# Attention backward: dQ in two 256-column matmuls, all of dS turned by the DMA crossbar, dQ half a group later

## The chip, the cores and the metric

The kernel runs on one core of a Trainium2 chip. The metric is the time of one execution on the device in microseconds (us), forward and backward in one launch; the median of repeated runs is compared. A profiled execution gives a trace of every instruction of the core's engines: TensorE (PE; its weight loads are PEld), VectorE (DVE), ScalarE (ACT), GpSimd (POOL) and SyncE (SP, which only issues DMAs here).

## What is computed

The function is one transformer block with adaptive layer norm (S = 2048 tokens, D = 512, 32 heads of 16) and its whole gradient. The outputs are the block's output and the gradients of the input, the weights and the conditioning vector. Cut to what matters here, the attention is

```python
scores = jnp.einsum('bhqd,bhkd->bhqk', q, k) * scale
p = _softmax(scores, axis=-1)
o = jnp.einsum('bhqk,bhkd->bhqd', p, v)
```

and its gradient is taken by `jax.vjp`. With dP the product of dO and V, the backward forms dS = p * (dP - rowsum), then dK = dS^T Q, dV = p^T dO and dQ = dS K. The change concerns dQ and the turning of dS that it needs.

## The kernel before

The program has three stretches: the forward with the backward of the MLP (0 to 1170 us), the attention backward (`attn_bwd`, L1429, 1170 to 2401 us) and the closing weight gradients and input gradient (`phase6`, to 2522 us). Only the second and the start of the third are touched.

**Loops.** `attn_bwd` walks over 8 quads of heads (g), 2 pairs of heads in each (jp), 4 chunks c of 512 keys and 16 blocks ib of 128 queries. Four query blocks make a group (G = 4), so a pair has 16 groups and the whole has 256. One step is one query block for the two heads a = 0, 1 of a pair. Queries are on the partitions, the 512 keys along the free dimension.

**One step** issues, for each head: the scores (L1584) into a PSUM tile `st` (three buffers); dP of the step before (`dP`, L1509) into a PSUM tile `dp` (three buffers); ScalarE's exponential of `st` into `pu` (L1587); and VectorE's product of `dp` and `pu` into the dS tile (L1513). The scores and dP use different halves of TensorE's rows. The dS tile `dsg` holds a group: 128 x (4 steps, 2 heads, 512 keys), from a pool of three buffers (L1354).

**The hand-over.** In every second group (`off`, L1515: the odd ones) the tile of step 1, head 1 isn't multiplied by VectorE: ScalarE copies `dp` to SBUF (L1521) and GpSimd multiplies (L1522). So VectorE has 7 products in an odd group and 8 in an even one.

**Batches.** After the two st and dP pairs of a step TensorE does a batch of older work: after odd steps dK and dV of two steps (`kv`, L1455: 8 matmuls of 512 columns on four column tiles), after even steps dQ of four units (`dq`, L1478). A unit of dQ is one 128-key block of one head of one group. For it, K's 32 columns (two heads' place, one of them zero) are the weights and the turned dS is the moving operand:

```python
for i in range(G):
    nc.tensor.matmul(accq[32 * i:32 * i + 32, ib0 // G, :], lhsT=T["K"][:, 4 * c + sub, col:col + 32],
                     rhs=dsT[:, (i * 2 + a) * 4 + sub, :],
```

So the four query blocks of a group lie on four strips of 32 PSUM partitions, and the group's number along the free dimension. All chunks accumulate in one PSUM tile `accq`.

**Turning dS.** `dsT` holds the group's 32 blocks of 128 x 128 with keys on the partitions (four buffers, L1355). In an odd group the DMA crossbar turns all 32 (`dma_start_transpose` on SyncE's queue, L1530, issued when the group's last product is issued). In an even group `turn_ds` (L1535) has TensorE transpose the first four blocks into an `st` buffer (L1543) and ScalarE copy them out (L1544), and the crossbar turns the other 28.

**When dQ runs.** `dS` appends 8 units to `pendq` when a group is complete. After an even step, four units are popped if more than 16 wait (eight if more than 24, L1595). In steady state 24 wait at a group's first step, so a batch reads a dsT whose turning was issued two groups before.

**The end of a pair.** With the pair's last unit, `dq` has VectorE scale `accq` into `dqT` (L1483) and appends a turn to `turnq`. A turn is popped at step 1 of a group (L1578), one in each: first two for dK and dV (`turn`, L1468 and L1472), then the one for dQ (`turn_q`, L1491: four transposes; L1492: one ScalarE copy). The last pair's rest is done after the loops (L1601 to L1629), among the first matmuls of the weight gradients.

The order on TensorE, SyncE and GpSimd in this stretch is the order of the code; nothing reorders it. GpSimd's queue also issues the loads of the next pair's operands (L1573), each behind a small copy (L1572) that paces it. `keep` (L1366) is a buffer of 128 x 8192: its first 2048 columns hold K of the even quads, and in the last pair all of it is filled with the normalised input for the weight gradients.

Of the kernel before, what the change touches and what calls it, by code (L numbers as in the profile page):

```python
# [9 lines left out]
BF16 = mybir.dt.bfloat16  # L10
F32 = mybir.dt.float32
ACT = mybir.ActivationFunctionType
ALU = mybir.AluOpType
# [6 lines left out]
P = 128  # L20
DH = 16
# [84 lines left out]
class K:  # L106
# [1230 lines left out]
    def phase5(self):  # L1337
        S, D, NQ, ST, DT = self.S, self.D, self.NQ, self.ST, self.DT
        nc, io = self.nc, self.io
        opa = self.open_pool("p56a", bufs=1)  # L1340
        self.pup = self.open_pool("p5pu", bufs=6)
        self.dq_t = opa.tile([P, ST, D], BF16, name="dq_t")
        self.dk_t = opa.tile([P, ST, D], BF16, name="dk_t")
        self.dv_t = opa.tile([P, ST, D], BF16, name="dv_t")
        self.opa = opa
        self.junk6 = opa.tile([P, D], F32, name="junk6")
        nc.gpsimd.memset(self.dsa_part[:], 0.0)
        assert ST * self.H == D
        self.cs = [self.csq[:], self.rl[:].rearrange("p s h -> p (s h)"), self.mod_25[:, 1, :]]
        self.parts = [self.dq_t, self.dk_t, self.dv_t]  # L1350
        self.stp = self.open_pool("p5st", bufs=3, space=PSUM)
        self.dpp = self.open_pool("p5dp", bufs=3, space=PSUM)
        self.kvp = self.open_pool("p5kv", bufs=1)
        self.dsp = self.open_pool("p5ds", bufs=3)  # L1354
        self.dtp = self.open_pool("p5dt", bufs=4)  # L1355
        self.accp = self.open_pool("p5acc", bufs=1, space=PSUM)
        self.attn_bwd()
# [71 lines left out]
    def attn_bwd(self):  # L1429
# [12 lines left out]
        accp = self.accp  # L1442
        acckv = accp.tile([P, 512], F32, name="acckv")
        nc.vector.memset(acckv[:], 0.0)
        accq = accp.tile([P, ST // G, P], F32, name="accq")
        masked, kvs = self.masked, self.kvs
        pend, pendq, turnq = [], [], []

# [25 lines left out]
        def dq(u):  # L1474
            (T, g, jp, c, ib0, a, sub, dsT) = u
            col = 32 * (2 * jp + a) - DH * a
            for i in range(G):
                nc.tensor.matmul(accq[32 * i:32 * i + 32, ib0 // G, :], lhsT=T["K"][:, 4 * c + sub, col:col + 32],  # L1478
                                 rhs=dsT[:, (i * 2 + a) * 4 + sub, :],
                                 start=(c == 0 and ib0 == 0 and a == 0 and sub == 0), stop=False,  # L1480
                                 skip_group_check=True)
            if (c, ib0, a, sub) == (SC - 1, ST - G, 1, 3):
                nc.vector.tensor_scalar(self.dqT[:], accq[:].rearrange("p b q -> p (b q)"), self.scale, None, ALU.mult)  # L1483
                turnq.append((g, jp, None, 0))

        def turn_q(g, jp):

            h0 = 4 * g + 2 * jp
            tp = stp.tile([P, ST // G, P], BF16, name="st")
            for b in range(ST // G):  # L1490
                nc.tensor.transpose(tp[:, b, :], self.dqT[:, b * P:(b + 1) * P], self.ident[:])  # L1491
            nc.scalar.copy(self.dq_t[:, :, h0 * DH:(h0 + 2) * DH], tp[:].rearrange("p b (i e) -> p (b i) e", i=G))  # L1492

        def kv_two(n=2):
            for u in pend[2 - n:2]:
# [19 lines left out]
        def off(c, ib):  # L1515
            return (c * SC + ib // G) % 2 == 1
# [7 lines left out]
        def dS(u):  # L1524

            (T, g, jp, c, ib, kvT, pu, dsg, i, grp) = u
            pend.append((T, g, jp, c, ib, kvT, pu, dsg[:, i]))
            if i == G - 1:
                dsT, n = grp
                nc.sync.dma_start_transpose(dsT[:, n:, :], dsg[:].rearrange("p i a k -> p (i a k)")[:, n * P:])  # L1530
# [17 lines left out]
        last = None  # L1548
        for g in range(NQ):
            for jp in range(2):  # L1550
                if jp == 0:
# [14 lines left out]
                for c in range(SC):  # L1566
                    c0 = 512 * c
                    for ib0 in range(0, ST, G):
                        m = c * (ST // G) + ib0 // G
                        while pieces and (total - len(pieces)) * SC * ST <= m * G * total:  # L1570
                            if last:
                                nc.gpsimd.tensor_copy(tick[:], last[7][0:1, 0, 0, 0:1])  # L1572
                            nc.gpsimd.dma_start(*pieces.pop(0))  # L1573
                        dsg, grp = self.dsp.tile([P, G, 2, 512], BF16, name="ds"), []
                        for i in range(G):
                            ib = ib0 + i
                            q = slice(ib * P, (ib + 1) * P)
                            if turnq and i == 1:  # L1578
                                turn(*turnq.pop(0))
                            pu = self.pup.tile([P, 2, 512], BF16, name="pu")  # L1580
                            for a in range(2):
                                stt = stp.tile([P, 512], F32, name="st")
                                rs = slice(64 * jp, 64 * jp + 64)
                                nc.tensor.matmul(stt[:], lhsT=T["QT"][rs, q], rhs=masked["KT"][a][rs, c0:c0 + 512],  # L1584
                                                 start=True, stop=True)
                                held = dP(last, a) if last else None
                                nc.scalar.activation(pu[:, a, :], stt[:], ACT.Exp, scale=self.scale)  # L1587
                                if held is not None:
                                    dP_pool(last, held)
                            if last:  # L1590
                                dS(last)
                            last = (T, g, jp, c, ib, kvT, pu, dsg, i, grp)
                            if i % 2 == 1 and len(pend) >= 4:
                                kv_two()
                            elif i % 2 == 0 and len(pendq) > 4 * G:  # L1595
                                for _ in range(8 if len(pendq) > 6 * G else 4):
                                    dq(pendq.pop(0))
                            if i == 2:
                                turn_ds(dsg, grp, off(c, ib))
            T = Tn  # L1600
        with tc.manual_schedule(engines=ALL):  # L1601
            for t in (2, 0):
# [339 lines left out]
```

## Time and profile before

| what | value |
|---|---|
| median of three runs | 2524.97 us (2520.79 to 2530.05) |
| the profiled execution, its span | 2524.31 us, 2522.4 us |
| mean granted TensorE clock | 0.998 |
| stretch 1170 to 2401 us: PE, DVE, ACT, POOL busy | 1192.3, 1186.4, 1207.2, 317.1 us of 1231 |
| GB/s of the DMAs in that stretch | 222 |
| crossbar issues (L1530), landing after min / median / max | 256; 5.3 / 7.1 / 10.2 us |
| ScalarE copies of turned blocks (L1544) | 128, 605 ns each |

In lines of groups the first number after the bar is the busy time in us, the second the mean length of one in ns; then comes the idle time of the engine just before them and what ended most of it. Lengths of neighbouring instructions overlap, since an engine starts one before the last has fully ended: the distance from start to start is the cost, not the length. For the same reason matmul busy time says little about how full TensorE is. Lines of the timeline give start, length from the first start to the last end, engine, code line, operation, operands and how many were merged. Everything that the prediction costs is in the stretch from 1170 to 2401 us and in the first 15 us behind it.

### The profile page before, as it was taken

The numbers are of one execution on the slowest core, as the hardware profiler recorded it, in microseconds if no ns is written. First come the engines' busy times: TensorE is split into PE (matmuls) and PEld (weight loads), VectorE is DVE, ScalarE is ACT, GpSimd is POOL, SyncE is SP. The second block draws the span as 40 slices with busy tenths as digits, with TensorE's granted clock in tenths as the row PEclk, the third lists the DMA queues.
The fourth block names the chain that finished last, engine by engine and source line by source line (L and its number), as shares of the span: only waits on it lengthen the run. The fifth ranks groups of instructions, "written<-read, shape, count | busy, mean of one in ns | idle before, by whom it ended". The sixth has DMA issues, their size and how long they took to land.

```text
span 2522.4 us, 76903 instructions
## 1 busy us (share of the span) xinstructions
PE 2433.1 (96%) x30791; PEld 1107.9 (44%) x30791; DVE 1705.4 (68%) x3519; ACT 2296.2 (91%) x3773; POOL 713.9 (28%) x1289
## 2 busy tenths in 40 slices
PE   8999999999999999989999999999999999999998
PEld 4555555555555554673333333333333333333343
DVE  6222223422332343667999999999999999999957
ACT  7999999999999997535999999999999999999945
POOL 2344531321131022255222222222222222222223
PEclk9999999999999999999999999999999999999999
DMA  4589761441343044699999999999999999999997
GB/s 167 134 178 202 179 114 64 116 99 44 103 118 74 24 137 129 139 191 214 234 221 218 218 226 220 223 227 218 219 218 223 225 221 221 222 228 226 237 211 198
DMA packets 1260558, 446.30 MB, mean 177 GB/s; under 512 B 1204052, under 2 KB 1228246, under 8 KB 1260198
## 3 DMA queue, kind: packets, MB, share of 16 engines
q1 hardware_dynamic: 1219654, 336.29, 70.7%
q0 software_dynamic: 38464, 104.04, 13.9%
q8 instruction: 241, 3.95, 0.7%
q10 hardware_dynamic: 2080, 1.05, 0.1%
q14 instruction: 119, 0.97, 0.1%
HBM read 75.83 MB, written 64.49 MB: 56 GB/s over the span
## 4 chain that ended last, share of the span: by engine, by line
PE 59%; ACT 22%; DMA 11%; issue 4%; DVE 3%; SPq 1%; POOL 0%; DVEq 0%; ACTq 0%; POOLq 0%
ACT pu L391 18%; PE st L1584 17%; DMA dsT<-ds 8%; PE acckv L1455 8%; PE st L388 8%; PE accq L1478 5%; PE accbank L322 3%; PE dp L1509 3%; ACT pu L1587 2%; PE dps L1050 2%; PE pps L1237 2%; PE dps L995 1%; DVE ds L1513 1%; PE st L1543 1%; PE pps L631 1%
## 5 line engine op out<-in xcount | busy, mean ns | idle before, releaser
L1513 DVE TENSOR_TENSOR ds<-dp,pu 128x512 bf16<-128x512 f32 x1920 | 1178.3, 681 | 44.5 <-PE dp L1509 26.4
L1587 ACT ACTIVATE pu<-st 128x512 bf16<-128x512 f32 x2048 | 1073.9, 641 | 39.4 <-PE st L1584 21.3
L391 ACT ACTIVATE pu<-st 128x1024 bf16<-128x1024 f32 x992 | 912.2, 1077 | 5.4 <-PE st L388 5.1
L388 PE MATMUL st<-QTm,KTq 128*128 128x512 bf16 x1984 | 588.4, 377 | 19.7 <-ACT pu L391 6.1
L322 PEld LDWEIGHTS <-pu 128*128 128x128 bf16 x8192 | 347.2, 96 | 236.2 <-issue 3.2
L322 PE MATMUL accbank<-Vaug,pu 128*128 128x17 bf16 x8192 | 357.6, 171 | 1.2 <-ACT Vaug L522 0.9
L1509 PE MATMUL dp<-kvm,q 64*128 64x512 bf16 x1024 | 356.4, 382 | 2.2 <-DVE g2w L1056 0.7
L1509 PE MATMUL dp<-kvm,dOTg 64*128 64x512 bf16 x1024 | 356.2, 382 | 0.9
L1584 PE MATMUL st<-kvm,QTg 64*128 64x512 bf16 x1024 | 327.2, 381 | 10.5 <-ACT pu L1587 7.4
L1584 PE MATMUL st<-kvm,q 64*128 64x512 bf16 x1024 | 326.6, 380 | 10.8 <-ACT pu L1587 7.6
L388 PEld LDWEIGHTS <-KTq 128*128 128x128 bf16 x1984 | 188.2, 96 | 177.5 <-issue 125.9
L1522 POOL TENSOR_TENSOR ds<-junk,pu 128x512 bf16<-128x512 f32 x64 | 73.7, 1151 | 378.6 <-DVE ds L1513 336.7
L1522 POOL TENSOR_TENSOR ds<-csq,pu 128x512 bf16<-128x512 f32 x64 | 73.8, 1154 | 356.6 <-ACT csq L1521 356.6
L302 POOL DMA_DIRECT2D QTm<-QTq_d x124 | 63.5, 514 | 342.7 <-PE st L388 321.3
L1455 PE MATMUL acckv<-ds,Qg 128*16 128x512 bf16 x1024 | 154.3, 381 | 0.0
L1455 PE MATMUL acckv<-pu,dOg 128*16 128x512 bf16 x1024 | 154.2, 381 | 0.0
L1455 PE MATMUL acckv<-pu,q 128*16 128x512 bf16 x1024 | 154.0, 381 | 0.0
L1455 PE MATMUL acckv<-ds,q 128*16 128x512 bf16 x1024 | 154.0, 381 | 0.0
L329 DVE RECIPROCAL rl<-accbank 128x4 f32<-128x4 f32 x128 | 22.9, 179 | 159.5 <-PE accbank L322 159.2
L1584 PEld LDWEIGHTS <-q 64*128 64x128 bf16 x1024 | 58.1, 94 | 137.9 <-issue 104.5
L1584 PEld LDWEIGHTS <-QTg 64*128 64x128 bf16 x1024 | 57.7, 94 | 137.7 <-issue 102.7
L1509 PEld LDWEIGHTS <-q 64*128 64x128 bf16 x1024 | 88.4, 93 | 64.2 <-issue 47.4
(387 smaller groups left out, 3138.6 us busy)
## 6 DMA issues: line engine op xcount, KB each, us to landing
KTq<-KTq_d POOLq DMA_DIRECT2D x24, 512.0 KB, 3.8
duT_d<-auT POOLq DMA_DIRECT2D x3, 1792.0 KB, 8.2
aT_d<-rT POOLq DMA_DIRECT2D x3, 1792.0 KB, 11.6
KTq_d<-KTq SPq DMA_DIRECT2D x32, 128.0 KB, 2.0
QTq_d<-ev_fm SPq DMA_DIRECT2D x32, 128.0 KB, 3.4
ktm_d<-ev_tm POOLq DMA_DIRECT2D x32, 128.0 KB, 2.5
VTq_d<-vT POOLq DMA_DIRECT2D x4, 1024.0 KB, 5.8
dsT<-ds SPq DMA_TRANSPOSE x256, 7.1
```

What stands on the lines that cost most here:

```text
L302: nc.gpsimd.dma_start(QTm[j][32 * j:32 * j + 32, :], self.QTq_d[g, 32 * j:32 * j + 32, 512 * qc:512 * (qc + 1)])
L322: nc.tensor.matmul(acc[:, a, sub, :], lhsT=pu[:, a, sub * P:(sub + 1) * P], rhs=Vaug[:, kb, h, :], start=(kb == 0 and a == 0 and sub == 0) ...
L388: nc.tensor.matmul(stt[:, a, :], lhsT=KT[:, kb * P:(kb + 1) * P], rhs=QTm[2 * jp + a][:], start=True, stop=True)
L391: nc.scalar.activation(pu[:], stt[:], ACT.Exp, scale=self.scale)
L1050: nc.tensor.matmul(pt[:], lhsT=a[st], rhs=g_tm[:, st, :], start=(st == 0), stop=(st == ST - 1))
L1455: nc.tensor.matmul(acckv[r:r + DH, :], lhsT=T[n][:, ib, col:col + DH], rhs=src[:, a, :], start=(ib == 0), stop=(ib == ST - 1))
L1478: nc.tensor.matmul(accq[32 * i:32 * i + 32, ib0 // G, :], lhsT=T["K"][:, 4 * c + sub, col:col + 32], rhs=dsT[:, (i * 2 + a) * 4 + sub, :], ...
L1509: nc.tensor.matmul(dp[:], lhsT=T["dOT"][rd, ib * P:(ib + 1) * P], rhs=masked["VT"][a][rd, 512 * c:512 * (c + 1)], start=True, stop=True)
L1513: nc.vector.tensor_tensor(dsg[:, i, a], dp[:], pu[:, a, :], ALU.mult)
L1522: nc.gpsimd.tensor_tensor(dsg[:, i, 1], f[:], pu[:, 1, :], ALU.mult)
L1584: nc.tensor.matmul(stt[:], lhsT=T["QT"][rs, q], rhs=masked["KT"][a][rs, c0:c0 + 512], start=True, stop=True)
L1587: nc.scalar.activation(pu[:, a, :], stt[:], ACT.Exp, scale=self.scale)
```

## The change

dQ's matmuls take 256 columns: two matmuls for each unit, each with two query blocks. Their place in `accq` follows: with b the group's number in the chunk, partitions 32 x (2 x (b mod 2) + h) and columns 256 x (b // 2). `turn_q` copies out in two parts accordingly. The crossbar turns all 32 blocks of every group except in the last pair, where even groups still go by TensorE and ScalarE. The dS tiles become a ring of three tiles and a fourth that lies in `keep`, behind K; in the last pair only the three are used. The bounds for popping dQ units rise from 16 and 24 to 20 and 28.

```diff
-        self.dsp = self.open_pool("p5ds", bufs=3)
+        dsp = self.open_pool("p5ds", bufs=1)
+        self.ds_ring = [dsp.tile([P, 8 * 512], BF16, name=f"ds{k}")[:] for k in range(3)]
+        self.ds_ring.append(self.keep[:, ST * P:ST * P + 8 * 512])
...
-        accq = accp.tile([P, ST // G, P], F32, name="accq")
+        accq = accp.tile([P, 512], F32, name="accq")
...
-            for i in range(G):
-                nc.tensor.matmul(accq[32 * i:32 * i + 32, ib0 // G, :], lhsT=T["K"][:, 4 * c + sub, col:col + 32],
-                                 rhs=dsT[:, (i * 2 + a) * 4 + sub, :],
-                                 start=(c == 0 and ib0 == 0 and a == 0 and sub == 0), stop=False,
+            b = ib0 // G
+            for h in range(2):
+                r, o = 32 * (2 * (b % 2) + h), 256 * (b // 2)
+                nc.tensor.matmul(accq[r:r + 32, o:o + 256], lhsT=T["K"][:, 4 * c + sub, col:col + 32],
+                                 rhs=dsT[:].rearrange("p (i w) k -> p i w k", i=G)[:, 2 * h:2 * h + 2, 4 * a + sub, :],
+                                 start=(c == 0 and b < 2 and a == 0 and sub == 0), stop=False,
...
-            nc.scalar.copy(self.dq_t[:, :, h0 * DH:(h0 + 2) * DH], tp[:].rearrange("p b (i e) -> p (b i) e", i=G))
+            for h in range(2):
+                nc.scalar.copy(self.dq_t[:, 8 * h:8 * h + 8, h0 * DH:(h0 + 2) * DH].rearrange("p (s i) e -> p s i e", i=2),
+                               tp[:, 2 * h:2 * h + 2, :].rearrange("p i (s e) -> p s i e", s=G))
...
-                        dsg, grp = self.dsp.tile([P, G, 2, 512], BF16, name="ds"), []
+                        ring = self.ds_ring[:3] if (g, jp) == (NQ - 1, 1) else self.ds_ring
+                        dsg, grp = ring[n_ds % len(ring)].rearrange("p (i a k) -> p i a k", i=G, a=2), []
+                        n_ds += 1
...
-                            elif i % 2 == 0 and len(pendq) > 4 * G:
-                                for _ in range(8 if len(pendq) > 6 * G else 4):
+                            elif i % 2 == 0 and len(pendq) > 5 * G:
+                                for _ in range(8 if len(pendq) > 7 * G else 4):
                                     dq(pendq.pop(0))
                             if i == 2:
-                                turn_ds(dsg, grp, off(c, ib))
+                                turn_ds(dsg, grp, (g, jp) != (NQ - 1, 1) or off(c, ib))
```

More of the change, by code (lines that the diff above doesn't have):

```diff
@@ L1476, in dq @@
             col = 32 * (2 * jp + a) - DH * a
-            for i in range(G):
-                nc.tensor.matmul(accq[32 * i:32 * i + 32, ib0 // G, :], lhsT=T["K"][:, 4 * c + sub, col:col + 32],
-                                 rhs=dsT[:, (i * 2 + a) * 4 + sub, :],
-                                 start=(c == 0 and ib0 == 0 and a == 0 and sub == 0), stop=False,
+            b = ib0 // G
[4 more added lines that the diff above has]
+                                 start=(c == 0 and b < 2 and a == 0 and sub == 0), stop=False,
                                  skip_group_check=True)
             if (c, ib0, a, sub) == (SC - 1, ST - G, 1, 3):
-                nc.vector.tensor_scalar(self.dqT[:], accq[:].rearrange("p b q -> p (b q)"), self.scale, None, ALU.mult)
+                nc.vector.tensor_scalar(self.dqT[:], accq[:], self.scale, None, ALU.mult)
                 turnq.append((g, jp, None, 0))
@@ L1529, in dS @@
                 dsT, n = grp
-                nc.sync.dma_start_transpose(dsT[:, n:, :], dsg[:].rearrange("p i a k -> p (i a k)")[:, n * P:])
+                nc.sync.dma_start_transpose(dsT[:, n:, :], dsg.rearrange("p i a k -> p (i a k)")[:, n * P:])
                 for a in range(2):
@@ L1547, in attn_bwd @@
         T = self.T0
-        last = None
+        last, n_ds = None, 0
         for g in range(NQ):
```

## The prediction

> **What bounds the kernel now.** I read the page first, for the shares and the groups; then the busy times of the stretch that the diff touches; then the waits of that stretch; then single stretches of the timeline, engine by engine. The profiled execution took 2524.3 us, 2522.4 of it in the span; the median of the three runs is 2525.0, so a sum made on the profile carries over as it is. The backward attention lies between 1170 and 2401 us. The page's groups, with busy time and mean length of one (engine and operation named):
>
> ```profile
> L1513 DVE TENSOR_TENSOR ds<-dp,pu 128x512 bf16<-128x512 f32 x1920 | 1178.3, 681 | 44.5 <-PE dp L1509 26.4
> L1587 ACT ACTIVATE pu<-st 128x512 bf16<-128x512 f32 x2048 | 1073.9, 641 | 39.4 <-PE st L1584 21.3
> ```
>
> VectorE's product is busy for 1178.3 us of these 1231 and idle for 44.5 us in all. The reader should see that nothing that spares ScalarE or TensorE work can bring more than those 44.5 us. The waits between 1176 and 2401 us (waiting line, what ended the wait, total, times, longest):
>
> ```profile
> DVE ds L1513 <- PE dp L1509: 26.4, 62, 2.0
> PE st L1584 <- ACT pu L1587: 14.9, 44, 0.5
> PE accq L1478 <- DMA dsT<-ds: 13.8, 22, 2.1
> DVE ds L1513 <- ACT pu L1587: 3.1, 11, 0.3
> ```
>
> VectorE waits almost only for TensorE's dP, hardly for ScalarE. The timeline of VectorE gives its pace: five products in a stretch with nothing in the way, then five around the tile that ScalarE and GpSimd take over (two answers, start and length first):
>
> ```profile
> 1797.74 3.07 DVE L1513 TENSOR_TENSOR ds<-dp,pu 128x512 bf16<-128x512 f32 x5
> ...
> 1800.73 3.39 DVE L1513 TENSOR_TENSOR ds<-dp,pu 128x512 bf16<-128x512 f32 x5
> ```
>
> One product lasts 0.68, so the first line is (3.07 - 0.68) / 4 = 0.598 us from start to start; the second loses 3.39 - 3.07 = 0.32. Two groups (one with the hand-over, one without) have 15 products: 15 x 0.598 = 8.97, plus 0.31 is 9.28 us. The crossbar's issues on SyncE repeat at just this distance:
>
> ```profile
> 1883.28 4.06 SPq L1530 DMA_TRANSPOSE dsT<-ds  x1
> ...
> 1888.02 3.59 SPq L1530 DMA_TRANSPOSE dsT<-ds  x1
> ...
> 1892.57 4.01 SPq L1530 DMA_TRANSPOSE dsT<-ds  x1
> ```
>
> 1892.57 - 1883.28 = 9.29. So the steady loop is VectorE plus 0.31. Where the 0.31 comes from is in TensorE's timeline:
>
> ```profile
> 1800.87 0.37 PE L1509 MATMUL dp<-kvm,q 64*128 64x512 bf16 x1
> 1801.17 0.41 PE L1478 MATMUL accq<-dsT,keep 128*32 128x128 bf16 x16
> ...
> 1801.51 0.39 PE L1509 MATMUL dp<-kvm,q 64*128 64x512 bf16 x1
> ...
> 1802.06 0.37 PE L1509 MATMUL dp<-kvm,q 64*128 64x512 bf16 x1
> 1802.36 0.39 PE L1455 MATMUL acckv<-ds,q 128*16 128x512 bf16 x2
> ...
> 1802.91 0.39 PE L1509 MATMUL dp<-kvm,q 64*128 64x512 bf16 x1
> ```
>
> A dQ batch (16 matmuls) takes 1801.51 - 1801.17 = 0.34 us of TensorE, a dK/dV batch (8 of 512 columns) 0.54. The dP at 1800.87 is the handed-over tile; the next dP stand behind the dQ batch, behind a dP buffer (1802.06) and behind the dK/dV batch (1802.91), and VectorE starts on each about 0.52 after it (1801.51 to 2.03).
>
> **What the Trainium skill says.** "TensorE: Matmul & The Clock Gate", Part 3 (The mechanism): column tiles of 32 run at once, each with its own weights. The trace agrees: 16 matmuls of 128 columns pass in 0.34 us. The same page, Back-to-back issue gap: N / 2.4 + 2.5 ns, so 56 ns for 128 columns and 109 for 256. The trace: 4 rounds in 0.34, 57 each with 0.11 around them. "DMA: Bandwidth & Descriptors", Latency and other measured facts: 261 GB/s for a DMA transpose; here 32 blocks of 32,768 bytes in 4.06 us are 258. "VectorE: DVE Perf Modes", Why PSUM operands drop a tier: fp32 from PSUM goes at one element a cycle, which fits 0.598 for 512, and no part of the diff changes that.
>
> **The change part by part.**
> *dQ in 256 columns.* Before, the four matmuls of a unit sat on four column tiles; now two matmuls of a unit use two tiles (rows 64 x (b mod 2) onwards), and all units of a batch have the same b. So a batch of 4 units streams 4 x 256 = 1024 columns after each other, as the dK/dV batch does: 0.54 instead of 0.34, +0.20 us in 512 batches, 102 us of TensorE. In the steady loop I put it against the recurrence above. X is the product whose end frees the buffer of the handed-over dP (start 1800.13). The first dP behind the batch would start at X + 1.58 instead of X + 1.38, its product at X + 2.10; but the third product behind it waits for X + 1.20 (the last before the hand-over) + 0.73 (its buffer free) + 0.30 + 0.54 (dK/dV batch) + 0.52 = X + 3.29 today, and by the new path for 2.10 + 2 x 0.598 = X + 3.30. A tie: the loss stays at 0.31. TensorE's sum for two groups is 8 x 0.535 (st and dP) + 4 x 0.54 + 4 x 0.54 = 8.6 of 9.28. Cost 0; if its cover goes, at most the whole 102; if a batch costs 0.02 more, 128 x 0.02 = 3. A gain is excluded, since TensorE only gets more.
> *The crossbar turns all.* 120 groups lose 4 transposes (0.33 of TensorE each) and a ScalarE copy that moves the next exponential by 0.46. ScalarE's sum for two groups falls from 16 x 0.477 + 2 x 0.46 = 8.55 to 8.09, both under 9.28: 0 in the steady loop. Around a pair's end, where the dK/dV copies crowd ScalarE, it may give 0 to 0.8 us; TensorE's longer batches stand in the same place, so I take 0.2 x 15 = -3. SyncE gets 4 blocks more in every second group, 4.06 against 3.59: 0.5 us per two groups, 8.1 of 9.28 where nothing disturbs.
> *Half a group later, fourth buffer.* A batch reads its dsT after 2.5 groups (11.6 us) instead of 2 (9.3); landings take 5.3 to 10.2. The 13.8 us of waits for the crossbar, in about eight spells, each get 2.3 us of credit, but in these spells (issues up to 5.2 us, with loads beside them) 4/60 more is moved, some 200 us x 0.067 = 13 us. Net -1, from -14 to +12. No VectorE wait for a dS buffer is in the trace: 0 for the buffer.
> *A new wait.* Before, the last dQ batch of a pair stood in the third group of the next pair, VectorE's scaling of accq followed in the crowd there, and the four transposes of dqT came three steps later:
>
> ```profile
> 1799.12 0.40 PE L1491 MATMUL st<-ident,dqT 128*128 128x128 bf16 x4
> ...
> 1799.45 0.39 PE L1509 MATMUL dp<-kvm,q 64*128 64x512 bf16 x1
> ```
>
> Now the last batch falls on the first step of the fourth group, and the transposes are popped in the very next step: in the changed program's order on TensorE they stand directly behind the last eight dQ matmuls. TensorE must wait until VectorE, with up to three dP tiles in front, has scaled accq; behind it in TensorE's queue stand the next st and dP, so VectorE runs dry. From the scaling's start: 0.73 until TensorE goes on (as from X to 1800.87), 0.33 for the transposes, 0.52 until the next product: 1.58, of which 0.60 is the scaling itself, done before too. Loss 1.0 us, at 15 ends of pairs: +15. Less is possible if VectorE catches up through the 0.8 above; more if ScalarE runs dry too (1.3).
> *Tail.* 28 units are left instead of 24, at 0.107 instead of 0.057: 3.0 - 1.4 = +1.6, on TensorE, which VectorE's last scaling waits for. dq_t in two copies instead of one: a tenth, 0.
> Sum: 0 - 3 - 1 + 15 + 1.6 = +12.6, 2524.3 + 12.6 = 2537.
>
> **Rivals.**
> A: the credit takes away all waits for the crossbar, 13.8: 2524.3 + 15 - 3 + 1.6 - 13.8 = 2524. For it: the longest wait is 2.1, under 2.3. Against: the spells are fed by more blocks.
> B, the faster side: ScalarE is the bound (91% busy on the page, TensorE waits 44 times for it). Then 120 x 0.46 = 55 go, and 2524.3 - 55 + 16.6 = 2486. It decides if the dP waits of VectorE come from st buffers held by ScalarE; only 14.9 us of TensorE's waits say so, and 8.55 is under 9.28.
> C: the crossbar becomes the bound in a third of the loop (43 double groups): at the disturbed pace of 9.9 us for 60 blocks, 4 more are 0.66: 28 on top of the waits and the tail, less what TensorE's wait gives back: 2524.3 + 28 + 5 = 2557.
> D: the longer batches are not covered: half of 102 shows, 2524.3 + 51 + 13.6 = 2589. Against: 8.6 under 9.28.
>
> **How the numbers follow.** My forecast (2528 to 2547) 0.52, A 0.20, B 0.11, C 0.12, D 0.05. About 0.3%, 7.6 us, is what a measurement can tell from no change. Slower by more: C, D and 0.44 of the forecast, 0.61; within: A but for 0.03, and the rest of the forecast, 0.25; faster: B and 0.03 of A, 0.14. The range leaves out B, D and a little of C and A: 2517 to 2553.
>
> **What would show it.** Right: the crossbar's issues still 9.28 apart for two groups; dQ batches of 0.54; once in each pair VectorE idle for about 1 us ahead of its first product of the fourth group, with TensorE waiting for VectorE at the transposes of dqT; few waits of accq for the crossbar. Wrong: a steady distance of 9.0 (ScalarE had mattered), or over 9.4 (batches or crossbar uncovered); no idle time at the transposes; waits of accq for dsT over 14 us.

## The result, and the profile after

The changed kernel takes 2563.19 us (median of four runs, 2562.92 to 2563.97), the kernel before 2523.49 in the runs beside it. The ratio is 1.0153 with a 95% interval of 1.0136 to 1.0171: slower by 1.5%, some 39 us. The forecast was 2537, +12.6. The direction is right; the size is three times what was forecast, and 2563 lies outside the forecast's range of 2517 to 2553.

The profiled execution has a span of 2561.7 us against 2522.4 before, so it shows the same 39 us, and it shows them in the stretch of the attention backward. An issue is one `dma_start_transpose` on SyncE's queue, and its length is the time that it holds this queue. From one crossbar issue to the issue 16 groups later (one pair of heads) the 15 first pairs take 79.7 us each, 76.9 before; 15 x 2.88 = 43. The last pair, where TensorE still turns a part, takes 72.2 us from its first issue to its last (73.0 before), and the first issue of all comes 3.0 us earlier in this trace: 43.2 - 0.8 - 3.0 is the 39 again.

The page's groups of the changed kernel (busy us, mean ns of one, then idle time before them). VectorE's product now has two rows, since the fourth buffer is called keep:

```profile
L1595 ACT ACTIVATE pu<-st 128x512 bf16<-128x512 f32 x2048 | 1085.7, 612 | 78.9 <-PE dp L1515 23.5
L1519 DVE TENSOR_TENSOR ds<-dp,pu 128x512 bf16<-128x512 f32 x1500 | 913.8, 680 | 44.1 <-PE dp L1515 34.7
...
L1519 DVE TENSOR_TENSOR keep<-dp,pu 128x512 bf16<-128x512 f32 x420 | 262.7, 681 | 49.7 <-PE dp L1515 44.8
```

One product is as long as before (0.68), but VectorE is idle for 44.1 + 49.7 = 93.8 us ahead of them, where it was 44.5. Half of it is ahead of the 420 products into keep, a fifth of all. The waits between 1170 and 2440 us (total, times, longest):

```profile
DVE keep L1519 <- PE dp L1515: 44.8, 59, 2.0
DVE ds L1519 <- PE dp L1515: 34.7, 86, 1.2
PEld L1495 <- DVE dqT L1487: 26.3, 15, 1.8
PE accq L1482 <- DMA dsT<-ds: 25.5, 32, 1.7
...
PE st L1495 <- DVE dqT L1487: 22.1, 15, 1.5
...
PE accq L1482 <- DMA dsT<-keep: 5.8, 11, 1.4
...
PE st L1592 <- ACT pu L1595: 0.7, 3, 0.3
```

Two things are new to TensorE: it waits for the scaling of dqT once in each of 15 pairs, up to 1.8 us, as forecast; and it waits for the crossbar 25.5 + 5.8 = 31.3 us, 13.8 before. The crossbar's own row says why. All issues on SyncE, by source (shortest, median and longest in ns), the kernel before first:

```profile
L1530 SPq DMA_TRANSPOSE dsT<-ds x256: 3419/4113/5953, 1176.1 to 2401.8; - x128
```

```profile
L1536 SPq DMA_TRANSPOSE dsT<-ds x196: 3517/4410/6452, 1173.1 to 2441.2; - x196
L1536 SPq DMA_TRANSPOSE dsT<-keep x60: 4882/5458/6605, 1187.7 to 2363.6; - x60
```

The shortest of the 60 issues that read the fourth buffer, 4.9 us, is longer than the median of the others, 4.4. Over the first 240 groups the mean issue grew from 4.20 to 4.86 us, and the issues fill 97.6% of the time, 87.4% before. In the timeline they stand end to end (start, length):

```profile
1799.42 4.71 SPq L1536 DMA_TRANSPOSE dsT<-ds  x1
...
1804.23 5.30 SPq L1536 DMA_TRANSPOSE dsT<-keep  x1
...
1809.62 14.01 SPq L1536 DMA_TRANSPOSE dsT<-ds  x3
```

1799.42 + 4.71 = 1804.13, and the next one starts 0.1 us later. So by this trace SyncE's queue, that is the crossbar, sets the pace; the experiments test it. The forecast had this as rival C, in a third of the loop; it is nearly the whole.

### The profile page after: what moved, and what is told of

The parts are those of the page before. It is cut to its first block, busy times and chain, and to the rows that moved or that the text cites. A ratio compares the mean times of both kernels' runs of the same rounds, so it can differ in the third digit from the quotient of the medians.

```text
span 2561.7 us, 67535 instructions
## 1 busy us (share of the span) xinstructions
PE 2455.1 (96%) x26215; PEld 1078.3 (42%) x26215; DVE 1705.2 (67%) x3519; ACT 2277.2 (89%) x3669; POOL 715.8 (28%) x1289
## 3 DMA queue, kind: packets, MB, share of 16 engines
q1 hardware_dynamic: 1281094, 352.02, 74.1%
q0 software_dynamic: 38464, 104.04, 13.8%
## 4 chain that ended last, share of the span: by engine, by line
PE 57%; ACT 19%; DMA 17%; DVE 3%; issue 3%; POOL 1%; SPq 0%; DVEq 0%; ACTq 0%; POOLq 0%
ACT pu L391 17%; PE st L1592 15%; DMA dsT<-ds 12%; PE st L388 8%; PE accq L1482 8%; PE acckv L1457 8%; PE accbank L322 3%; PE dp L1515 2%; DMA dsT<-keep 2%; PE dps L1050 2%; PE pps L1237 2%; PE dp L1643 1%; DVE ds L1519 1%; PE pps L631 1%; PE st L1738 1%
## 5 line engine op out<-in xcount | busy, mean ns | idle before, releaser
L1519 DVE TENSOR_TENSOR ds<-dp,pu 128x512 bf16<-128x512 f32 x1500 | 913.8, 680 | 44.1 <-PE dp L1515 34.7
L1592 PE MATMUL st<-kvm,QTg 64*128 64x512 bf16 x1024 | 313.5, 381 | 0.9 <-ACT pu L1595 0.5
L1592 PE MATMUL st<-kvm,q 64*128 64x512 bf16 x1024 | 313.5, 382 | 0.5 <-ACT pu L1595 0.3
L1519 DVE TENSOR_TENSOR keep<-dp,pu 128x512 bf16<-128x512 f32 x420 | 262.7, 681 | 49.7 <-PE dp L1515 44.8
L1482 PE MATMUL accq<-dsT,keep 128*32 128x256 bf16 x2048 | 157.1, 275 | 16.1 <-DMA dsT<-ds 12.4
L1482 PE MATMUL accq<-dsT,Kg 128*32 128x256 bf16 x2048 | 155.9, 275 | 16.5 <-DMA dsT<-ds 13.6
L1528 POOL TENSOR_TENSOR keep<-csq,pu 128x512 bf16<-128x512 f32 x60 | 69.3, 1156 | 353.3 <-ACT csq L1527 353.3
L1482 PEld LDWEIGHTS <-keep 128*32 128x32 bf16 x2048 | 83.6, 95 | 134.5 <-issue 130.0
L1482 PEld LDWEIGHTS <-Kg 128*32 128x32 bf16 x2048 | 82.9, 95 | 130.3 <-issue 125.5
L1592 PEld LDWEIGHTS <-q 64*128 64x128 bf16 x1024 | 57.9, 94 | 166.3 <-issue 153.9
```

What stands on the lines that cost most here:

```text
L1482: nc.tensor.matmul(accq[r:r + 32, o:o + 256], lhsT=T["K"][:, 4 * c + sub, col:col + 32], rhs=dsT[:].rearrange("p (i w) k -> p i w k", i=G) ...
L1519: nc.vector.tensor_tensor(dsg[:, i, a], dp[:], pu[:, a, :], ALU.mult)
L1528: nc.gpsimd.tensor_tensor(dsg[:, i, 1], f[:], pu[:, 1, :], ALU.mult)
```

## Experiments

The first theory after the result: the crossbar is the bound, because the fourth buffer starts at byte 204,768 of its partition in the built program, 224 past a multiple of 256, while the three other buffers start on multiples. Rivals: the additional blocks alone (crossbar's volume), and the new wait at the turn of dQ. In the table, "pair" is the mean distance of 16 crossbar issues in the first 15 pairs, "issue" their mean length, both from one trace each. A trace is of one execution: the same program in those pairs differed by 0.8 us a pair between two traces (e14 and e18), and the traced execution lies 7 to 8 us above the median of its runs in e8, e16 and e18 and 13 below it in e12. e13 and e14 compute a wrong dQ in the last pair, as told below.

| run | ratio to before, 95% interval | pair, us | issue, us |
|---|---|---|---|
| before | 1 | 76.9 | 4.20 |
| changed kernel | 1.0153 (1.0136 to 1.0171) | 79.7 | 4.86 |
| e1 aligned | 1.0092 (1.0072 to 1.0111) | 78.4 | 4.65 |
| e2 later turn | 1.0158 (1.0138 to 1.0179) | 79.5 | 4.85 |
| e3 both | 1.0041 (1.0020 to 1.0062) | 77.6 | 4.67 |
| e4 both, 128 columns | 1.0145 (1.0130 to 1.0160) | 79.6 | 4.87 |
| e5 before, buffers shifted | 1.0598 (1.0546 to 1.0649) | 86.3 | 5.23 |
| e6 before + crossbar turns all | 1.0121 (1.0105 to 1.0138) | 78.7 | 4.67 |
| e7 before + 256 columns | 1.0096 (1.0074 to 1.0118) | 78.5 | 4.04 |
| e8 before + later dQ and turn | 0.9997 (0.9984 to 1.0010) | 77.3 | 4.28 |
| e9 both, half crossbar | 1.0088 (1.0056 to 1.0120) | 78.4 | 4.10 |
| e10 both, matmuls split | 1.0141 (1.0113 to 1.0169) | 79.5 | 4.82 |
| e11 both, 32 idle a group | 1.0110 (1.0091 to 1.0129) | 78.5 | 4.76 |
| e12 both, 96 idle a group | 1.0160 (1.0142 to 1.0178) | 78.0 | 4.73 |
| e13 four strips, half (dQ wrong) | 1.0196 (1.0174 to 1.0218) | 76.5 | 4.15 |
| e14 four strips, all (dQ wrong) | 1.0264 (1.0232 to 1.0296) | 77.4 | 4.57 |
| e15 later turn, three buffers | 1.0080 (1.0065 to 1.0095) | 78.4 | 4.69 |
| e16 before + 256 + all | 1.0117 (1.0094 to 1.0140) | 78.2 | 4.46 |
| e17 four strips, half, mended | 1.0014 (1.0004 to 1.0024) | 76.6 | 4.14 |
| e18 four strips, all, mended | 1.0085 (1.0068 to 1.0102) | 78.2 | 4.60 |

**The alignment of the buffer (e1, e5).** e1 puts the fourth buffer 32 bytes further, on a multiple of 256:

```diff
-        self.ds_ring.append(self.keep[:, ST * P:ST * P + 8 * 512])
+        self.ds_ring.append(self.keep[:, ST * P + 16:ST * P + 16 + 8 * 512])
```

> The changed kernel with one edit: the fourth dS buffer begins 32 bytes later inside keep, so that its SBUF address is a multiple of 256 (204,800 instead of 204,768). In the changed kernel a crossbar issue from keep takes 5.43 us on the mean, one from the three other dS buffers 4.45 to 4.90. Theory 1 (the place of the source makes the crossbar slow): issues from keep fall to the others' length, about 4.6, some 0.8 x 60 = 48 us of crossbar time go, and the time falls to 2520 to 2540. Theory 2 (32 blocks in every group are more than the crossbar carries, wherever they lie): issues stay, 2560 +- 5. Theory 3 (TensorE's wait at the transposes of dqT is the loss): 2560 +- 5, and the wait of 1.7 us at 15 ends of pairs stays.

Measured: 2547.75 us, 15 us less than the changed kernel and 8 above the range of theory 1. Its crossbar row:

```profile
L1536 SPq DMA_TRANSPOSE dsT<-ds x196: 3595/4420/7538, 1174.8 to 2422.0; - x196
L1536 SPq DMA_TRANSPOSE dsT<-keep x60: 3928/4310/6258, 1189.4 to 2345.8; - x60
```

The issues from keep are now like the others, as theory 1 said; that less time came of it than forecast shows that the address isn't all. e5 is the reverse: the kernel before with its three dS buffers 32 bytes past a multiple of 256, by a small tile ahead of them in the pool.

```diff
-        self.dsp = self.open_pool("p5ds", bufs=3)
+        dsp = self.open_pool("p5ds", bufs=1)
+        dsp.tile([P, 16], BF16, name="pada")
+        self.ds_ring = [dsp.tile([P, 8 * 512], BF16, name=f"ds{k}")[:] for k in range(3)]
...
```

> The kernel before, with nothing of the change, only its three dS buffers placed 32 bytes past a multiple of 256 (as the fourth buffer of the changed kernel is). Theory of alignment: every crossbar issue becomes longer by 0.8 to 0.9 us (the mean of 4.36 for 32 blocks goes to about 5.2, that of 28 blocks from 4.0 to about 4.8), two groups then need about 10 us of SyncE in place of 8.4, and the crossbar sets the pace: about 128 times 0.7 more, some 2610 us (2590 to 2625). Rival, that the fourth buffer was slow for its place among the other tiles and not for its alignment: issues as before, 2524 to 2528 us.

```profile
L1533 SPq DMA_TRANSPOSE dsT<-ds x256: 4173/5042/9586, 1175.3 to 2549.0; - x128
```

Measured: 2671.28 us, 46 past the range expected; the median issue went from 4.11 to 5.04. The expectation says that the fourth buffer lies the same way. It doesn't: it lies 32 bytes short of a multiple, that is 224 past one, so e5 tries a second shift. Its page counts the same packets and bytes on the crossbar's queue as the kernel before (1219654, 336.29 MB), so only the address differs. The Trainium skill ("DMA: Bandwidth & Descriptors", How a descriptor splits into AXI transactions) says that a transaction must start at a 256-byte boundary, so a piece of 256 bytes that doesn't takes two. The blocks that the change gives to the crossbar add 352.02 - 336.29 = 15.73 MB in 1281094 - 1219654 = 61440 packets to its queue, 256 bytes each, and both shifts cost about the same: 0.8 us an issue at 224 bytes (the mean of the issues from keep is 5.43 in the changed kernel, 4.64 in e1), 1.0 at 32 bytes (5.23 in e5, 4.20 before). That agrees with a count of transactions, two in place of one in both. By bytes fetched (an estimate from that page: 9 beats of 32 bytes in place of 8 at a shift of 32, and 15 in place of 8 at 224) the shift by 224 should cost several times more. That the address sets the length is shown; that it does so by the number of transactions is not.

**The new wait (e2, e3).** The turn of dQ goes from step 1 of the group to step 3, so that it doesn't stand right behind the last dQ batch:

```diff
-                            if turnq and i == 1:
+                            if turnq and i == (3 if turnq[0][2] is None else 1):
```

The place in question in the changed kernel (start, length):

```profile
1579.70 0.61 PE L1482 MATMUL accq<-dsT,keep 128*32 128x256 bf16 x8
...
1581.06 0.68 DVE L1487 TENSOR_SCALAR dqT<-accq 128x512 bf16<-128x512 f32 x1
...
1581.79 0.40 PE L1495 MATMUL st<-ident,dqT 128*128 128x128 bf16 x4 [1.48 <-DVE dqT L1487]
...
1582.74 0.69 DVE L1519 TENSOR_TENSOR keep<-dp,pu 128x512 bf16<-128x512 f32 x1 [1.01 <-PE dp L1515]
```

TensorE stands still until VectorE has scaled; VectorE's next product then comes 1.68 after the scaling's start (1.58 in the forecast), idle for 1.0 of it (1.0 in the forecast).

> The changed kernel with one edit: the turn of dQ is popped at step 3 of a group instead of step 1, two steps behind VectorE's scaling. TensorE's wait for the scaling (48 us in the profile of the changed kernel, 15 times) should vanish in any case. Theory 3: the time falls by 15 to 25, to 2540 to 2548. Theories 1 and 2 (the crossbar sets the pace, and catches up while TensorE waits): it falls by less than 8.

> Both edits, the aligned fourth buffer and the later turn. Theory 1 with theory 3 behind it: the two together take more than the two alone, since with the crossbar free the wait at the transposes is exposed: 2508 to 2522, at or under the kernel before. Theory 2: 2550 or more.

Measured: the wait is gone in both traces. (The 48 us in the expectation of e2 add the two rows of one wait, of the weight load and of the matmul; it is 22 to 26 us.) Alone that gives nothing (e2, 2563.82), as theories 1 and 2 said: the crossbar is late anyway, and the pause only let it catch up. On top of the alignment it gives 11.7 us more (e3, 2536.09), near the 15 x 1.0 of the forecast. But e3 lies between its two intervals: theory 1 said at most 2522, and 14 us more are left.

**The parts alone and together (e6, e7, e8, e16, e15, e9).** e6 has only the last line of the diff (`turn_ds` skipped outside the last pair), e7 only the new `dq`, `accq` and `turn_q`, e8 only the bounds 20 and 28 with the later turn of e2, e16 the edits of e6 and e7.

> The kernel before with the crossbar turning all of dS outside the last pair, and nothing else: three buffers, dQ in four strips, its distance and its turn as before. Theory of the crossbar's volume: four blocks more in every other group with the fetches of the 128-column dQ fill SyncE as in the run with both mends and four strips (2563 us); with less distance for dQ rather more: 2558 to 2580 us. Rival, that TensorE sets the pace and its 60 times 4 transposes spared (3 us a pair between the undisturbed pairs of the runs with and without them) decide: 2485 to 2510 us.

> The kernel before with dQ in two matmuls of 256 columns alone; crossbar, buffers, distance of dQ and turn as before. Theory of fetches: 32 fetches of instructions fewer in the backward loop (180 to 148), crossbar issues 0.05 us shorter in the mean, and since SyncE has 8 us free in a pair of heads nearly nothing of it is seen: 2517 to 2526 us. Rival, that TensorE's longer batches lie open where half of the turning is TensorE's too: up to 0.2 us a group, 2540 to 2550 us.

> The kernel before with dQ half a group later and the turn of dQ one step later, and nothing else. If the waits of dQ for the crossbar in the kernel before (13.8 us) are worth their length, they go and the time is 2508 to 2516 us. Rival, that the work that takes their place on TensorE finds its operands no earlier (the pair of heads is bound by TensorE's and ScalarE's own work): 2520 to 2528 us.

e6 took 2553.83 us, a little under the lower end expected of the crossbar's volume, and far from the rival. Its crossbar row and wait:

```profile
L1530 SPq DMA_TRANSPOSE dsT<-ds x256: 3962/4568/6705, 1177.0 to 2431.0; - x128
```

```profile
PE accq L1478 <- DMA dsT<-ds: 61.5, 90, 1.7
```

All buffers are aligned here, and still the mean issue is 4.67 us: two make 9.34, more than the 9.28 of the steady loop. e7 took 2549.55, where the theory of the moment said no cost and the rival, TensorE's longer batches lying open, said this: the rival's time came. In its trace the pair is longer everywhere, not in spells (a pair undisturbed, that is the median over the pairs of each of its 16 distances, summed: 78.4 us against 76.2 before), and dQ waits only 5.5 us for the crossbar. e8 took 2522.49, no difference that can be measured:

```profile
DVE ds L1513 <- DMA dsT<-ds: 6.3, 8, 2.1
...
PE accq L1478 <- DMA dsT<-ds: 2.3, 1, 2.3
```

The waits of dQ for the crossbar went from 13.8 to 2.3 us, as the credit of half a group says. But now VectorE waits 6.3 us for a dS buffer that the same late crossbar still reads, and no time was won. (This trace is of an execution 7 us above the median, so it shows where the late crossbar is felt, not the price.)

> The kernel before with 256 columns and the whole of dS on the crossbar, neither the later dQ nor the fourth buffer. Theory that the two parts offset each other (fewer fetches for the crossbar, four transposes fewer beside TensorE's longer batches): 2530 to 2545 us, far under the sum of the two alone (2580). Rival, that the offset came from the later dQ: 2560 to 2580 us.

> The changed kernel with the later turn and three dS buffers, all aligned, without the fourth. Forecast's step that the buffer is worth nothing: as with the aligned fourth buffer, 2530 to 2541 us. Rival, that with a crossbar nearly full the fourth buffer lets VectorE run ahead over a late transpose: 2545 to 2560 us, with waits of VectorE for the transposes.

e16: 2550.69, 6 us past the upper end of the first theory, but far under the sum of e6 and e7 (30.5 + 24.2): the two parts cancel most of each other even without the later dQ. e15 is e3 without the fourth buffer (`ring = self.ds_ring[:3]`); 2542.11, between the two intervals, 1 us past what the forecast's zero allowed, with the wait that the rival named:

```profile
DVE ds L1519 <- DMA dsT<-ds: 12.9, 15, 2.4
```

So an aligned fourth buffer is worth about 10 us once the crossbar is full (1.0080 to 1.0041), and the buffer as the change places it costs about 20 against none (1.0158 of e2 to 1.0080).

> The changed kernel with the fourth buffer aligned and the turn of dQ one step later, and the crossbar turning as before (TensorE turns the quarter of every other group). Theory of the crossbar's volume: the run with both and the whole of dS on the crossbar has 39 us in its 15 pairs above its own undisturbed pair of 75.0 us, from crossbar issues that come late; with 28 blocks in place of 32 in every other group SyncE is free for some 4 us more in a pair, and 20 to 30 us of the 39 come back: 2505 to 2516 us. Rival, that TensorE with its four transposes back and the longer dQ batches sets the pace: the pair goes to 77 to 78 us undisturbed and the time to 2540 to 2560.

e9 (in e3, `turn_ds(dsg, grp, off(c, ib))`) took 2543.42, in the rival's interval. Its pairs have little disturbance but 78.1 us undisturbed, about as in e7; when the crossbar takes the four transposes the undisturbed pair falls to 75.4 (e3). What is slow in e7 and e9 stands in their waits. VectorE's wait for ScalarE's exponential, in e7, e9 and e3:

```profile
DVE ds L1517 <- ACT pu L1591: 30.4, 86, 0.4
```

```profile
DVE ds L1519 <- ACT pu L1595: 29.9, 77, 0.4
```

```profile
DVE ds L1519 <- ACT pu L1595: 4.9, 18, 0.4
```

It was 3.1 us before, and the 27 us more are about what e7 and e9 cost (24 and 22). In e7 68 of the 79 such waits in the 15 first pairs are at VectorE's first product behind the handed-over tile. The wait needs both the long batches and a part of the turning on TensorE and ScalarE: with short batches it is 3.1 (before) and 2.3 (e6), with long ones and all on the crossbar 8.8 (e16). What makes the exponential late at that place wasn't separated.

**Why 128 columns cost under a full crossbar (e4, e10, e11, e12).** e4 is e3 with dQ as before the change:

```diff
-            for h in range(2):
...
+            for i in range(G):
+                nc.tensor.matmul(accq[32 * i:32 * i + 32, ib0 // G, :], lhsT=T["K"][:, 4 * c + sub, col:col + 32],
+                                 rhs=dsT[:, (i * 2 + a) * 4 + sub, :],
...
```

> As the run with both edits, and dQ back at four matmuls of 128 columns on four column tiles (0.34 us a batch instead of 0.54). If the longer batches are hidden behind VectorE, as the prediction had it, the time is that of the run with both edits within 4 us; if they are not, it is lower by 10 to 50.

It took 2563.44, 27 us more than e3, although TensorE's batch is shorter: neither of its two expectations. A reading of the traces gave a new theory. The queues named instruction carry pieces of the program, 16 KB each on q8. In a least-squares fit over the issues of the loop (with the loads beside them as a second term), an issue with such a piece in its time is longer by 0.46 us before, 0.68 in the changed kernel and 0.79 in e3. With 256 columns dQ has 32 instructions fewer in a group (16 matmuls and 16 weight loads in place of 32 and 32), 8192 in 256 groups, and q8 has 205 pieces in place of 237. The Trainium skill ("Runtime: NRT & Kernel Launch", Instruction fetch mechanics) says that programs stream in blocks of 16 KiB, 256 instructions, by DMA, mostly hidden. The count agrees (8192 / 256 = 32 = 237 - 205). The hiding doesn't hold for a neighbour: by the fit, what the fetch delays here is the crossbar. e10 splits each matmul of 256 columns of e3 in two of 128, on the same two strips:

```diff
-            for h in range(2):
+            for k, h in ((0, 0), (0, 1), (1, 0), (1, 1)):
...
+                                 rhs=dsT[:, (2 * h + k) * 8 + 4 * a + sub, :],
```

> The changed kernel with the fourth buffer aligned and the later turn, and each dQ matmul of 256 columns given as two of 128 in the same 32 columns of the array: as many instructions as with four strips of 128 columns, but still two strips at a time. Theory of fetches: about 175 fetches in the loop in place of 148, each 0.4 us of crossbar issue, 2547 to 2565 us (2536 without the split, 2563 with four strips). Rival, that four strips read dS at once and so slow the crossbar's writes: 2533 to 2541 us, with fetches up and issue lengths by number of fetches as with 256 columns.

2561.56, as e4 and as the theory of fetches said. It isn't the four strips at once, nor the length of a batch (the median is 0.556 us of TensorE in e10, 0.546 in e3 and 0.340 in e4): it goes with the number of instructions. The some 30 pieces more are 24 us of crossbar by the fit. The issues of the 15 pairs are longer by 0.20 x 240 = 47 us in e4 and by 37 in e10, and the rest of that isn't explained. e11 and e12 leave TensorE as in e3 and give GpSimd instructions that do nothing, 8 and 24 at each step:

```diff
+                            for _ in range(8):
+                                nc.gpsimd.engine_nop()
```

> The changed kernel with the fourth buffer aligned and the later turn (2536 us), with 8 instructions that do nothing on GpSimd at each query tile of the backward loop, 32 a group: as many more as the 128-column dQ has on TensorE. Theory of fetches: GpSimd's instructions come in pieces of 16 KB over the same DMA engines, 32 pieces more, and each makes a crossbar issue 0.4 us longer with up to 0.7 us of time behind it: 2549 to 2558 us, and the issue means by number of fetches stay at 4.3, 4.9, 5.1. Rival, that it was TensorE's own longer stream (its weight loads, its waits for instructions) which cost the 25 us: 2533 to 2539 us.

> The same with three times as many idle instructions, 24 at each query tile, some 96 more fetches. Theory of fetches: in proportion, 40 to 70 us more than without, 2576 to 2606 us. Rival: 2533 to 2541 us, as GpSimd has time for them (28% busy).

The instruction queues of e4 (q8 alone), e3, e11 and e12 (packets, MB, share of 16 engines):

```profile
q8 instruction: 237, 3.88, 0.6%
```

```profile
q8 instruction: 205, 3.36, 0.6%
...
q14 instruction: 117, 0.96, 0.1%
```

```profile
q8 instruction: 205, 3.36, 0.5%
q14 instruction: 181, 1.48, 0.2%
```

```profile
q8 instruction: 205, 3.36, 0.6%
q14 instruction: 309, 2.53, 0.3%
```

GpSimd's pieces are of 8 KB, 64 and 192 more, where the page has 16 KiB for every engine. e11 took 2552.01 and e12 2562.29: by the ratios 17 and 30 us over e3, where the rival allowed 5 at most. e11 is in the interval of the theory, with twice the pieces at half the size. e12 missed its 40 to 70, since the expectation counted pieces of 16 KB; 192 pieces of 8 KB at the 0.17 us of the fit are 32. GpSimd isn't late for its own work: its product starts 0.08 us after ScalarE's copy in e3 and 0.09 in e12 (mean of 128; at most 0.31). So work that does nothing, on an engine that is 28% busy, costs 1.2%. That it costs this by the crossbar is what the fit says; the distances of e12's trace show little of it, since the traced execution is the fastest of its four (2549.36 us, the others 2562 to 2568).

**Strips (e13, e14, e17, e18).** To have few instructions and short batches, the units of two neighbouring groups are taken in turn, so that four matmuls on four strips run at once. That needs a fifth dsT, which lies aligned in keep in place of the fourth dS buffer:

```diff
-                        pendq.append((T, g, jp, c, ib - G + 1, a, sub, dsT))
+                        half.append((T, g, jp, c, ib - G + 1, a, sub, dsT))
+                if len(half) == 16:
+                    pendq.extend(u for two in zip(half[:8], half[8:]) for u in two)
+                    half.clear()
...
```

> dQ in 256 columns, but the units of two neighbouring groups in turn, so that four matmuls on four strips of the array run at once; dS in three buffers, a fifth dsT (aligned, in keep), the crossbar as before (TensorE turns four blocks in every other group, the last pair apart). Theory that 256 columns alone cost 25 us by the batch of 0.54 us on two strips: with four strips the batch is as short as before (2 rounds of 0.11 plus 0.11: 0.33), and the cost goes: 2512 to 2526 us. Rival, that the 256-column matmul itself or the new place of the rows costs: 2540 to 2550 us.

> The same with the crossbar turning all of dS. Theory of fetches: beside the crossbar part alone with 128 columns (2554 us) there are 28 pieces of 16 KB fewer, each worth about 0.8 us of crossbar: 2526 to 2536 us. Rival, that in that run the four strips at once slow the crossbar: they are there again, 2548 to 2558 us.

In both the last pair has only four dsT, too few for the distance, so that dQ there reads dS of other groups, which makes it wrong, and waits for them; the last pair took 122.7 and 125.7 us in place of 73, and the whole time says nothing on the theories. e17 and e18 take the last pair in plain order.

> 256 columns on four strips (units of two neighbouring groups in turn), a fifth dsT, the crossbar as before; the last pair in plain order with four dsT. Theory that 256 columns alone cost 25 us by the batch on two strips: 15 pairs at 76.5 us as in the kernel before, 2512 to 2525 us. Rival, that the matmul of 256 columns costs in itself: 2540 to 2550 us.

> The same with the crossbar turning all of dS outside the last pair. Theory of fetches: 28 pieces of 16 KB fewer than in the crossbar part alone (2554 us), some 0.8 us each: 2527 to 2536 us. Rival, that the four strips at once slow the crossbar in that run: 2548 to 2558 us.

e17 took 2526.62, 2 us past the theory's interval and far from the rival's. Its 15 pairs take 76.6 us as forecast; the last one, with two strips, takes 77.8 (73.0 before). One batch and TensorE's next work behind it, in the changed kernel and in e17:

```profile
1803.43 0.61 PE L1482 MATMUL accq<-dsT,Kg 128*32 128x256 bf16 x8
1803.98 0.39 PE L1592 MATMUL st<-kvm,q 64*128 64x512 bf16 x1
```

```profile
1805.31 0.29 PE L1483 MATMUL accq<-keep 128*32 128x256 bf16 x2
...
1805.64 0.40 PE L1554 MATMUL st<-ident,ds 128*128 128x128 bf16 x4
```

That is 0.55 and 0.33 us of TensorE, and VectorE's wait for the exponential is back at 4.9 us. So the 24 us of e7 were the batch on two strips, not the wide matmul. (e17 also reads dQ later; e8 says that this alone is worth nothing.) e18 took 2545.78, between the two expectations: by the ratios 9 us less than e6, not the 22 that 28 pieces of 16 KB at 0.8 would give. 4 of the missing 13 are its last pair (77.7 us, 73.6 in e6). What else it costs (dQ there reads from two groups, and the order differs) wasn't separated. No version was faster than the kernel before; e8 and e17 come closest.

## Why the forecast was wrong, step by step

The runs make a ladder from the kernel before to the changed one. Each rung is one part, but for the third, which is two (times are ratios times 2524; a rung is uncertain by 4 to 7 us, so the -1 is no difference):

| state | over before, us | this edit |
|---|---|---|
| crossbar turns all (e6) | +30.5 | +30.5 |
| and 256 columns (e16) | +29.5 | -1 |
| and later dQ, turn at step 3 (e15) | +20.2 | -9 |
| and a fourth buffer, aligned (e3) | +10.3 | -10 |
| and the turn at step 1 (e1) | +23.2 | +13 |
| and the buffer as placed (changed kernel) | +38.6 | +15 |

The rungs hold in this order only: what a part costs depends on the parts that are there already, as the bullets show.

- *The crossbar turns all*, -3: this step failed. It put SyncE at "8.1 of 9.28 where nothing disturbs", from issues read in a quiet place (4.06 and 4.01), and treated the disturbed places as a small correction elsewhere. In the kernel before, the 32-block issues of the 15 pairs take 3.93 to 5.66 us, 4.36 in the mean. With all blocks on the crossbar the mean is 4.67 (e6), so two groups need 9.34 and the room was not there. In the kernel before, the part costs 30 us. Rival C (28 on top) had the right mechanism; that its number fits is in part luck, since it counted a third of the loop. The gain that the step looked for does exist elsewhere: beside 256 columns the part costs nothing that can be told (+5, e7 to e16), and with the later dQ, the later turn and the aligned buffer as well it saves some 12 us (e9 to e3, uncertain by 10).
- *Half a group later, fourth buffer*, "0 for the buffer": failed. As placed it costs 15 (changed kernel to e1) to 28 us (e2 to e3) against an aligned one, because its address makes 60 issues 0.8 us longer, 48 us of crossbar time. Aligned it is worth about 10, since VectorE does wait for dS buffers as soon as the crossbar is late. "No VectorE wait for a dS buffer is in the trace" held for the kernel before only. The rest of the step, the later dQ at -1, came out by itself (e8, -0.8, with the later turn), but not as reckoned: by its trace the waits only change their place.
- *A new wait*, +15: the mechanism, its place and its length (1.0 us, 15 times) were right, and it costs 13 us where the crossbar leaves room (e3 to e1). In the changed kernel it costs nothing (e2), as the crossbar is behind anyway. Rival C had said that such a wait gives something back.
- *dQ in 256 columns*, 0: not one number. Alone it costs 24 us (e7), with the crossbar turning all nothing that can be told (e6 to e16, -1), and in e3 it saves 27 (e4 to e3); in the changed kernel itself it wasn't tested. The tie in the recurrence doesn't hold while TensorE and ScalarE still turn a part (the wait for the exponential, 30.4 us). And "a gain is excluded, since TensorE only gets more" is wrong: 8192 instructions fewer spare the crossbar some 25 us (e3 against e4 and e10).
- *Tail*, +1.6: not seen. From the last crossbar issue to the end the two traces have 120.5 us, 120.6 before.
- The signs named for a wrong forecast came: pairs at 78.3 us undisturbed, 9.8 for two groups (over 9.4), and 31.3 us of accq waiting for dsT (over 14). So did two of those named for a right one: batches of 0.55 us where 0.54 was forecast, and VectorE idle for 1.0 behind the scaling of dqT. Rival B is refuted by e6, which spares ScalarE the same copies and is slower; its 55 us were also more than the 44.5 which the prediction itself gave as the most that could be won.

Put together, the two mends of e3 take away what the forecast had as the wait and what it didn't have, the address. Without its wait the forecast stands at 12.6 - 15 = -2.4, and e3 is at +10.3: as far as the runs tell, those 13 us are the room on the crossbar that it had too large, and the 15 us of the address come on top.

What stays open: how much of the 10 us left in e3 is volume and how much is loads and fetches beside it, what makes the exponential late in e7, and 9 of the 13 us that e18 lacks.

## What to carry to other kernels

Before giving a queue more work, take its mean and its spread over the whole stretch, not an undisturbed instance: here 87% full with issues from 3.4 to 6.0 us left no room for 7% more blocks. Look at the byte address of every buffer that the crossbar reads, above all of a view cut out of another tile. And once a resource is full, costs that were hidden (an address, a fetch) show, while waits elsewhere become free: test each part alone and beside the others, since here one part cost 24 us alone and saved 27 in company.

## What was not expected of the hardware

- A crossbar transpose of 28 or 32 blocks of 128 x 128 takes about 0.8 to 1.1 us longer when its source starts 32 or 224 bytes past a multiple of 256: 5.04 against 4.11 us in the median (e5 and before), 5.46 against 4.31 (the issues from keep in the changed kernel and e1).
- A fetch of instructions beside a crossbar transpose lengthens it: by the fits 0.4 (e7) to 0.9 us (e10, e12) for a piece of 16 KB and 0.1 to 0.3 for one of 8 KB. 24,576 instructions that do nothing on GpSimd cost 30 us (e12 against e3).
- Eight matmuls of 256 columns on two strips of 32 take TensorE 0.55 us, on four strips 0.33 (changed kernel and e17).
